# Attention before two MLP layers: queries stored like keys, and one transpose for the last 64 queries and keys of a pair of heads

## The chip, the cores and the metric

One NeuronCore of a Trainium2 chip runs the whole program as one launch. The metric is the device time of one execution in microseconds (us). Before the change it is 1063.98 us, the median of three runs (1063.94, 1063.98, 1067.12).

## What is computed

The reference is attention with capped scores, whose output is the input of two MLP layers (called moe and moe2 there):

```
scores = cap * tanh((q @ k^T / sqrt(64)) / cap)
attn   = exp(scores) / sum(exp(scores))
x  = attn @ v                 # [4 batches, 12 heads, 448, 64], then laid out as 1792 tokens x 768
h  = x @ w_in                 # 768 -> 2048
x  = (h - tanh(h)) @ w_out    # 2048 -> 768
h  = x @ w_in2
out = (h * sigmoid(1.702 h)) @ w_out2
```

There are 4 x 12 = 48 heads of 448 queries and 448 keys, each with 64 elements. All inputs that matter here are fp32.

## The kernel before

The attention stage works on 24 pairs of heads, numbered g = 0 to 23 (`NG = 24`); a pair puts 2 x 64 = 128 features on the partitions. For a pair it does the following.

- `load_qk(g)` (L458) loads queries and keys as rows into a tile `raw`. The queries stand in 112 partitions with 4 consecutive rows of each head in a partition (`C = 4`, `CP = 112`). The first 384 keys stand in 128 partitions with 3 rows each (`KC = 3`), and the last 64 keys (`KT = 64`) in 64 partitions. That is five DMAs: two for the queries (L466), two for the keys (L472), one for the last 64 keys (L476). All are issued by SyncE (SP), one after the other; of pair 0 alone, one query load, one key load and the load of the last keys are issued by ScalarE. Three `raw` tiles exist, so `load_qk(g)` may start once the transposes of pair g - 3 are through.
- `prep_q(g)` (L500) transposes the four query blocks of 112 rows on TensorE (L506) into one PSUM bank, and VectorE copies 448 columns to the first half of a tile `qk` (L90). `prep_k(g)` (L509) transposes three key blocks of 128 rows (L515) and the block of 64 rows (L516), and another copy fills the second half.
- `scores` (L519) multiplies a block of 128 keys with all queries, separately for the two heads: 64 partitions each (L527). `tail_scores` (L530) does the last 64 keys of two pairs together (L537). ScalarE applies tanh and exp (L546, L548). `pair_pv` (L561) multiplies with the values (L568), and `sums_of_two` (L570) adds up the exponentials (L575).
- `load_v` (L485) loads the values of a pair in two DMAs (`rv` and `vt`).

The order on each engine follows the program for all that is wrapped in `pin`. In the loop over g (L648), the transposes of pair g + 3 stand in iteration g: ahead of `scores(g + 1, 0)` where g is even, and ahead of `pair_pv(g, 0)` where g is odd. Pairs 0, 1 and 2 are prepared ahead, and iteration 1 prepares pairs 3 and 4 right behind each other (L682). The load of pair g + 4 is written in iteration g (L686). TensorE works in this order and waits at the first instruction whose input isn't there.

SP issues all loads and stores of the stage in one queue: beside `raw`, `rv` and `vt` these are the weights of the first MLP layer (`wd`, L190, converted by ScalarE at L205 and VectorE at L214 and L220), the converted weights that are kept (`kept`, L241), attention output for later (`xd`, L586), the sums (`wrow`, L604) and their inverses read back as rows (`wb`, L610), which VectorE multiplies with at L655. The order in which SP issues them is set by the scheduler when the program is built.

The order of a pair's queries goes through the whole kernel as the order of the tokens. It is undone when the result is stored: `rows_out` (L1210) takes a block of 128 tokens and cuts it where a run of 112 ends, so every block is stored in two DMAs, each to rows 4 apart.

Of the kernel before, what the change touches and what calls it, by code (L numbers as in the profile page):

```python
# [9 lines left out]
F32 = mybir.dt.float32  # L10
# [30 lines left out]
def attention_moe_moe(ctx, tc, q, k, v, cap, w_in1, w_out1, w_in2, w_out2, out):  # L41
    nc = tc.nc
    B, H, S, D = q.shape
    DM, DF = w_in1.shape
    P = 128
    C = 4
    CP = S // C
    KC = S // P
    KT = S - KC * P
    NP = H // 2  # L50
    KM = DM // P
    KF = DF // P
# [4 lines left out]
    HW = DM // 2  # L57
# [19 lines left out]
    def pin(ins):  # L77
        return tc.keep_in_program_order(ins) if pinned[0] else ins
# [10 lines left out]
    def hi_dve(dst, src):  # L89
        pin(nc.vector.tensor_copy(out=dst, in_=src))  # L90
# [4 lines left out]
    ident = const.tile([P, P], F32, name="ident")  # L95
# [9 lines left out]
    xd = [dr_p.tile([P, TOKENS[1]], F32, name=f"xd{i}") for i in range(KM)]  # L105
    wrow = [dr_p.tile([4, NP // 2, n], F32, name=f"wrow{p}") for p, n in enumerate(TOKENS)]
    x_big = big.tile([P, 2 * KM * TOKENS[0]], F32R, name="x")
# [5 lines left out]
    def first_pool(name, bufs, **kw):  # L113
        return first.enter_context(tc.tile_pool(name=name, bufs=bufs, **kw))

    one_p = first_pool("one", 1)
    raw_p = first_pool("raw", 3)
# [12 lines left out]
    SR = P // 4  # L130
    sel = one_p.tile([P, NP // 2, SR], F32, name="sel")
    vt = [one_p.tile([P, P], F32, name=f"vt{i}") for i in range(4)]
# [228 lines left out]
    def add(out, a, kind, b):  # L361
        nc.vector.tensor_tensor(out=out, in0=a, in1=b, op=kind)  # L362
# [82 lines left out]

    NG = B * NP
    raw, rawv, qkt = {}, {}, {}
# [10 lines left out]
    def load_qk(g, second=None):  # L458
        if g >= NG:
            return  # L460
        b, hp = divmod(g, NP)
        t = raw_p.tile([P, 2, 2 * C * D], F32, tag="raw", name="raw")
        queues = (nc.sync, second or nc.sync)
        for j in range(2):
            a = slice(j * D, (j + 1) * D)
            queues[j].dma_start(  # L466
                out=t[:CP, 0].rearrange("p (c e) -> p c e", c=C)[:, :, a],
                in_=q[b, 2 * hp + j].rearrange("(p c) d -> p c d", c=C),
            )
        for j in range(2):  # L470
            a = slice(j * D, (j + 1) * D)
            queues[j].dma_start(  # L472
                out=t[:, 1].rearrange("p (c e) -> p c e", c=C)[:, :KC, a],
                in_=k[b, 2 * hp + j, :KC * P].rearrange("(p c) d -> p c d", c=KC),
            )
        queues[1].dma_start(  # L476
            out=t[:KT, 1, KC * P:].rearrange("p (h d) -> p h d", h=2),
            in_=k[b, 2 * hp:2 * hp + 2, KC * P:].rearrange("h p d -> p h d"),
        )
        raw[g] = t  # L480

    def tail_rows(g):
        return slice(g % 2 * KT, (g % 2 + 1) * KT)

    def load_v(g):  # L485
        if g >= NG:
            return
        b, hp = divmod(g, NP)
        tv = rv_p.tile([P, 2, KC, D], F32, tag="rv", name="rv")
# [10 lines left out]
    def prep_q(g):  # L500
        if g >= NG:
            return
        qkt[g] = st_p.tile([P, 2 * S], F32, tag="qk", name="qk")
        ps = ps_s.tile([P, 512], F32, tag="s", name="ps_qk")
        for c in range(C):
            pin(nc.tensor.transpose(ps[:, c * CP:(c + 1) * CP], raw[g][:CP, 0, c * P:(c + 1) * P], ident[:CP, :CP]))  # L506
        hi_dve(qkt[g][:, :S], ps[:, :S])

    def prep_k(g):  # L509
        if g >= NG:  # L510
            return
        ps = ps_s.tile([P, 512], F32, tag="s", name="ps_qk")
        t = raw.pop(g)
        for c in range(KC):
            pin(nc.tensor.transpose(ps[:, c * P:(c + 1) * P], t[:, 1, c * P:(c + 1) * P], ident))  # L515
        pin(nc.tensor.transpose(ps[:, KC * P:S], t[:KT, 1, KC * P:], ident[:KT, :KT]))  # L516
        (hi_act if g == 0 else hi_dve)(qkt[g][:, S:], ps[:, :S])

    def scores(g, c):  # L519
        if g >= NG:  # L520
            return
        ps = ps_b.tile([P, 2, 512], F32, tag="b", name="ps_sc")
        qk = qkt[g]
        kc = slice(S + c * P, S + (c + 1) * P)
        for j in range(2):
            a = slice(j * D, (j + 1) * D)
            pin(nc.tensor.matmul(ps[:, j, :S], qk[a, kc], qk[a, :S], start=True, stop=True))  # L527
        sc_t[g, c] = ps

    def tail_scores(g):  # L530
        if g >= NG:
            return
        ps = ps_b.tile([P, 2, 512], F32, tag="b", name="ps_tl")
        for n in (g, g + 1):
            for j in range(2):
                a = slice(j * D, (j + 1) * D)
                pin(nc.tensor.matmul(  # L537
                    ps[tail_rows(n), j, :S], qkt[n][a, S + KC * P:], qkt[n][a, :S], start=True, stop=True
                ))
        sc_t[g, KC] = ps  # L540

# [28 lines left out]
    def sums_of_two(g):  # L570
        b, p = divmod(g // 2, NP // 2)
        if p == 0:
            sum_t[b] = ps_r.tile([P, 512], F32, tag="r", name="ps_r")
        for n in range(4):
            pin(nc.tensor.matmul(  # L575
                sum_t[b][n * SR:(n + 1) * SR, :S], sel[:, p], ts_t[g + n // 2][:, n % 2],
                start=(p == 0), stop=(p == NP // 2 - 1),
            ))
# [38 lines left out]
    def attention():  # L617
# [5 lines left out]
        def x_part(n):  # L623
            b, i = divmod(n, NP)
            n = S if b == 0 else CUT
            return i, n, slice(b * S, b * S + n)

        load_qk(0, nc.scalar)
        nc.sync.dma_start(out=capr, in_=cap.partition_broadcast(P))
        nc.vector.tensor_scalar(  # L630
            out=cpos.bitcast(U32), in0=capr.bitcast(U32), scalar1=0x7FFFFFFF, scalar2=None, op0=ALU.bitwise_and
        )
        nc.vector.reciprocal(out=tsc, in_=cpos)
        nc.vector.tensor_scalar(out=tsc, in0=tsc, scalar1=QK_SCALE, scalar2=None, op0=ALU.mult)
        load_qk(1)
        load_v(0)
        load_qk(2)
        load_v(1)

        def prep(g):  # L640
            prep_q(g)
            prep_k(g)
# [110 lines left out]
    def part_of(tag, name="part"):  # L753
        return temp_p(tag).tile([P, NT if tag == "t" else TC], F32, tag=tag, name=name)[:, :TOKENS[now[0]] // 2]
# [455 lines left out]
    def rows_out(half, n, ps, plus=None, two=False):  # L1210
        tag = ("q", "v", "t", "far")[n % 4]
        o = part_of(tag, "o")[:, :HW]
        if plus is None:
            nc.scalar.copy(out=o, in_=ps[:, :HW])
        else:
            add(o, ps[:, :HW], ALU.add, plus)
        a0 = a = FIRST[now[0]] + n * P
        while a < a0 + P:
            z = min((a // CP + 1) * CP, a0 + P)
            s, c = divmod(a // CP, C)  # L1220
            p0 = a % CP
            dst = out[s * S:(s + 1) * S, half * HW:(half + 1) * HW].rearrange("(p c) e -> c p e", c=C)
            q = nc.scalar if two and a > a0 else nc.sync
            q.dma_start(out=dst[c, p0:p0 + z - a], in_=o[a - a0:z - a0])
            a = z

    def x_load(h, i):
# [104 lines left out]
```

## Time and profile before

| | |
|---|---|
| median of three runs | 1063.98 us |
| the profiled execution | 1063.42 us |
| its span, first to last instruction | 1061.6 us |
| TensorE (PE) busy | 1051.6 us, 99% |
| VectorE (DVE) busy | 811.6 us, 76% |
| ScalarE (ACT) busy | 692.3 us, 65% |
| GpSimd (POOL) busy | 54.5 us, 5% |
| shares of the chain that ended last | PE 92%, DVE 3%, DMA 1%, ACT 1% |
| of these, by line | L506 1%, L515 1%, L527 5%, L568 7% |

The attention stage takes about the first 200 us; the MLP layers take the rest. The profiled execution is 0.56 us faster than the median. A busy time counts an engine as busy while any of its instructions runs. TensorE's weight loads stand apart as PEld. Names such as `ps_qk` or `raw` are those of the program's tiles.

### The profile page before, as it was taken

The page shows a single profiled execution, that of the slowest core. Times are in us where ns is not written, and L with a number is a line of the kernel's source. Part 1 is how long each engine was busy: PE and PEld are TensorE (multiplying, and loading weights), DVE is VectorE, ACT ScalarE, POOL GpSimd, SP SyncE. Part 2 cuts the span into 40 slices and gives each one's busy share as a digit, 9 for nine tenths or more (in the row PEclk, how much of TensorE's full clock was granted, in tenths as well). Part 3 has the DMA queues.
Part 4 walks back from the last instruction along what each step waited for, and adds up shares of the span by engine and source line. Part 5 has one row for each costly group of instructions (what it writes and reads, how often), then busy time and mean ns, then how long its engine had stood idle before and what let it go on. Part 6 is the DMA issues. An engine that isn't in the chain of part 4 may idle for free.

```text
span 1061.6 us, 15403 instructions
## 1 busy us (share of the span) xinstructions
PE 1051.6 (99%) x5483; PEld 860.4 (81%) x5483; DVE 811.6 (76%) x1089; ACT 692.3 (65%) x958; POOL 54.5 (5%) x56
## 2 busy tenths in 40 slices
PE   9999999999999999999999999999999999999998
PEld 3333333699999998888878888887899999999998
DVE  4688979799985525988999998576799973448973
ACT  6898898798863425656785756655755755557663
POOL 0013243200000000000000000000000000000000
PEclk9999999999999999999999999999999999999999
DMA  6877668675577878887874853799654554444443
GB/s 145 210 204 210 193 185 239 202 245 212 190 241 246 296 247 267 280 300 247 274 232 144 272 191 90 262 320 301 226 166 132 182 160 125 136 120 142 150 136 103
DMA packets 153749, 218.17 MB, mean 206 GB/s; under 512 B 58380, under 2 KB 101704, under 8 KB 153672
## 3 DMA queue, kind: packets, MB, share of 16 engines
q1 hardware_dynamic: 152376, 216.58, 64.7%
q8 instruction: 43, 0.70, 0.3%
q10 hardware_dynamic: 1296, 0.61, 0.2%
q14 instruction: 34, 0.28, 0.1%
HBM read 158.86 MB, written 58.28 MB: 205 GB/s over the span
## 4 chain that ended last, share of the span: by engine, by line
PE 92%; DVE 3%; DMA 1%; ACT 1%; issue 1%; SPq 0%; DVEq 0%; ACTq 0%
PE ps_o L1182 19%; PE ps_h L900 19%; PE ps_h L1080 18%; PE ps_y L940 9%; PE ps_y L993 9%; PE ps_pv L568 7%; PE ps_sc L527 5%; PE ps_qk L506 1%; PE ps_tl L537 1%; PE ps_r L575 1%; PE ps_qk L515 1%; DMA wd<-in_moe_w_in_dram 1%; DVE wl L93 1%; DVE gr L800 0%; PE wps L1276 0%
## 5 line engine op out<-in xcount | busy, mean ns | idle before, releaser
L81 ACT CAST rh<-gr 128x512 fp32r<-128x512 f32 (+1 forms) x179 | 103.6, 584 | 101.8 <-PE ps_o L1182 63.3
L900 PE MATMUL ps_h<-x,wh 128*128 128x384 f32 (+1 forms) x672 | 152.9, 358 | 0.0
L93 DVE TENSOR_TENSOR rl<-gr,rh 128x512 fp32r<-128x512 f32 (+1 forms) x179 | 113.3, 638 | 25.7 <-ACT rh L81 24.8
L1182 PE MATMUL ps_o<-wh,rl 128*128 128x384 f32 x392 | 130.9, 334 | 0.0
L1182 PE MATMUL ps_o<-wh,rh 128*128 128x384 f32 x392 | 130.9, 334 | 0.0
L1182 PE MATMUL ps_o<-wl,rh 128*128 128x384 f32 x392 | 130.9, 334 | 0.0
L900 PEld LDWEIGHTS ps_h<-x,wh 128*128 128x128 f32 x672 | 121.1, 188 | 12.0 <-issue 0.7
L93 DVE TENSOR_TENSOR wl<-whole,wh 128x768 fp32r<-128x768 f32 (+1 forms) x103 | 93.7, 910 | 14.9 <-ACT wh L81 14.0
L81 ACT CAST wh<-whole 128x768 fp32r<-128x768 f32 (+1 forms) x103 | 82.4, 800 | 23.1 <-PE ps_h L1080 10.6
L1080 PE MATMUL ps_h<-x,wh 128*128 128x384 f32 (+1 forms) x336 | 97.2, 359 | 0.0
L900 PE MATMUL ps_h<-x,wl 128*128 128x384 f32 (+1 forms) x384 | 88.1, 364 | 0.0
L546 ACT ACTIVATE t<-ps_sc,tsc 128x896 f32<-128x896 f32 x72 | 69.8, 1004 | 22.4 <-PE ps_sc L527 22.4
L900 PEld LDWEIGHTS ps_h<-x,wl 128*128 128x128 f32 x384 | 69.8, 188 | 9.7 <-issue 1.4
L1182 PEld LDWEIGHTS ps_o<-wh,rh 128*128 128x128 f32 x392 | 73.6, 188 | 0.0
L1182 PEld LDWEIGHTS ps_o<-wl,rh 128*128 128x128 f32 x392 | 73.6, 188 | 0.0
L1182 PEld LDWEIGHTS ps_o<-wh,rl 128*128 128x128 f32 x392 | 73.6, 188 | 0.0
L548 ACT ACTIVATE t<-t,cpos 128x896 f32<-128x896 f32 x72 | 72.3, 1042 | 0.4
L1080 PE MATMUL ps_h<-x,wl 128*128 128x512 f32 (+1 forms) x192 | 69.5, 362 | 0.0
L362 DVE TENSOR_TENSOR gr<-gr 128x512 f32<-128x512 f32 (+2 forms) x112 | 68.9, 640 | 0.7 <-DMA gr<-xa 0.4
L527 PE MATMUL ps_sc<-qk 64*128 64x448 f32 x288 | 67.9, 570 | 0.8 <-ACT qk L81 0.6
L362 DVE TENSOR_TENSOR part<-ps_h,part 128x512 f32<-128x512 f32 (+1 forms) x48 | 29.8, 621 | 50.6 <-PE ps_h L1080 50.5
L220 DVE SCALAR_TENSOR_TENSOR wr<-wr,wd 128x768 uint32<-128x768 uint32 x48 | 46.1, 961 | 27.8 <-ACT wd L212 21.4
(154 smaller groups left out, 2193.9 us busy)
## 6 DMA issues: line engine op xcount, KB each, us to landing
wd<-in_moe_w_in_dram SPq DMA_DIRECT2D x64, 384.0 KB
wd<-in_moe_w_out_dram SPq DMA_DIRECT2D x29, 768.0 KB
whole<-single SPq DMA_DIRECT2D x36, 384.0 KB
whole<-s SPq DMA_DIRECT2D x33, 384.0 KB
wh<-kept SPq DMA_DIRECT2D x25, 384.0 KB
wl<-kept SPq DMA_DIRECT2D x25, 384.0 KB
single<-wr SPq DMA_DIRECT2D x24, 384.0 KB
whole<-t SPq DMA_DIRECT2D x22, 384.0 KB
```

What stands on the lines that cost most here:

```text
L81: pin(nc.scalar.copy(out=dst, in_=src))
L93: return pin(nc.vector.tensor_tensor(out=dst, in0=src, in1=hi.bitcast(F32), op=ALU.subtract))
L362: nc.vector.tensor_tensor(out=out, in0=a, in1=b, op=kind)
L527: pin(nc.tensor.matmul(ps[:, j, :S], qk[a, kc], qk[a, :S], start=True, stop=True))
L546: pin(nc.scalar.activation(out=t, in_=ps[:, :, :S], func=AF.Tanh, scale=tsc))
L548: ins = pin(nc.scalar.activation(out=tt[g, c], in_=tt[g, c], func=AF.Exp, scale=cpos))
L568: pin(nc.tensor.matmul(ps[a, :S], w, t[:, j], start=(c == 0), stop=(c == KC - 1)))
L900: pin(nc.tensor.matmul(ps, w[:, kk, :], x[kk][:, a], start=(m == 0), stop=(m == len(seq) - 1)))
L940: nc.tensor.matmul(bank[e][:, :a1 - a0], w[:, kk, c], x[2 * j + kk][:, a0:a1], start=(j == 0 and m == 0), stop=(j == KF // 2 - 1 and m == ...
L993: nc.tensor.matmul(ps[e], w[:, kk, c], x, start=(name == head and k == 0 and m == 0), stop=(k == KH - 1 and m == 2), skip_group_check=True,)
L1080: nc.tensor.matmul(ps, w, x, start=(name == head and m == 0), stop=(m == len(seq) - 1), skip_group_check=True,)
L1182: nc.tensor.matmul(ps[n], x[:, t], w[:, kk, :], start=(first and k == 0 and m == 0), stop=(k == KH - 1 and m == 2), skip_group_check=True,)
```

## The change

Queries are laid out as the keys are: 384 queries in 128 partitions with 3 rows each, and the last 64 apart. The last 64 queries and the last 64 keys of a pair share one block of `raw`: queries in partitions 0 to 63, keys in 64 to 127. One transpose of 128 x 128 turns both, so a pair has seven transposes of one shape where it had eight of three shapes. The first PSUM bank now holds 512 columns (448 queries and the 64 last keys) and the second 384. A pair's load has six DMAs where it had five, since the last queries are loaded by themselves; of pair 0, the load of the last keys moves from ScalarE's queue to SP's, and that of the last queries takes its place. `rows_out` cuts its blocks of 128 tokens at 128, 256, 384 and 448 of a batch, so 56 stores become 44.

```diff
-    C = 4
-    CP = S // C
     KC = S // P
     KT = S - KC * P
+    KQ0 = S + KT
...
-        t = raw_p.tile([P, 2, 2 * C * D], F32, tag="raw", name="raw")
+        t = raw_p.tile([P, 2 * KC + 1, 2 * D], F32, tag="raw", name="raw")
         queues = (nc.sync, second or nc.sync)
-        for j in range(2):
-            a = slice(j * D, (j + 1) * D)
-            queues[j].dma_start(
-                out=t[:CP, 0].rearrange("p (c e) -> p c e", c=C)[:, :, a],
-                in_=q[b, 2 * hp + j].rearrange("(p c) d -> p c d", c=C),
+        for n, (x, c0) in enumerate(((q, 0), (k, KC + 1))):
+            for j in range(2):
+                queues[j].dma_start(
+                    out=t[:, c0:c0 + KC, j * D:(j + 1) * D],
+                    in_=x[b, 2 * hp + j, :KC * P].rearrange("(p c) d -> p c d", c=KC),
+                )
+            queues[1 - n].dma_start(
+                out=t[n * KT:(n + 1) * KT, KC].rearrange("p (h d) -> p h d", h=2),
+                in_=x[b, 2 * hp:2 * hp + 2, KC * P:].rearrange("h p d -> p h d"),
             )
...
-        for c in range(C):
-            pin(nc.tensor.transpose(ps[:, c * CP:(c + 1) * CP], raw[g][:CP, 0, c * P:(c + 1) * P], ident[:CP, :CP]))
-        hi_dve(qkt[g][:, :S], ps[:, :S])
+        for c in range(KC + 1):
+            pin(nc.tensor.transpose(ps[:, c * P:(c + 1) * P], raw[g][:, c], ident))
+        hi_dve(qkt[g][:, :KQ0], ps)
...
-            pin(nc.tensor.transpose(ps[:, c * P:(c + 1) * P], t[:, 1, c * P:(c + 1) * P], ident))
-        pin(nc.tensor.transpose(ps[:, KC * P:S], t[:KT, 1, KC * P:], ident[:KT, :KT]))
-        (hi_act if g == 0 else hi_dve)(qkt[g][:, S:], ps[:, :S])
+            pin(nc.tensor.transpose(ps[:, c * P:(c + 1) * P], t[:, KC + 1 + c], ident))
+        (hi_act if g == 0 else hi_dve)(qkt[g][:, KQ0:], ps[:, :KC * P])
...
-        kc = slice(S + c * P, S + (c + 1) * P)
+        kc = slice(KQ0 + c * P, KQ0 + (c + 1) * P)
...
-                    ps[tail_rows(n), j, :S], qkt[n][a, S + KC * P:], qkt[n][a, :S], start=True, stop=True
+                    ps[tail_rows(n), j, :S], qkt[n][a, S:KQ0], qkt[n][a, :S], start=True, stop=True
...
-            z = min((a // CP + 1) * CP, a0 + P)
-            s, c = divmod(a // CP, C)
-            p0 = a % CP
-            dst = out[s * S:(s + 1) * S, half * HW:(half + 1) * HW].rearrange("(p c) e -> c p e", c=C)
+            s, t = divmod(a, S)
+            c = t // P
+            z = min(s * S + min((c + 1) * P, S), a0 + P)
+            dst = out[s * S:(s + 1) * S, half * HW:(half + 1) * HW]
+            if c < KC:
+                dst = dst[:KC * P].rearrange("(p c) e -> c p e", c=KC)[c]
+                t -= c * P
             q = nc.scalar if two and a > a0 else nc.sync
-            q.dma_start(out=dst[c, p0:p0 + z - a], in_=o[a - a0:z - a0])
+            q.dma_start(out=dst[t:t + z - a], in_=o[a - a0:z - a0])
```

On TensorE, VectorE, ScalarE and GpSimd the instructions stand in the same order as before, with the shapes changed and one transpose less per pair. The place on TensorE where iteration 1 prepares pairs 3 and 4 (`raw_380` and `raw_386`) before `pair_pv(1, 0)` reads, before:

```order
L506 MATMUL ps_qk_426<-ident_75,raw_380 128x112 x4
L515 MATMUL ps_qk_432<-ident_75,raw_380 128x128 x3
L516 MATMUL ps_qk_432<-ident_75,raw_380 128x64
L506 MATMUL ps_qk_439<-ident_75,raw_386 128x112 x4
L515 MATMUL ps_qk_445<-ident_75,raw_386 128x128 x3
L516 MATMUL ps_qk_445<-ident_75,raw_386 128x64
L568 MATMUL ps_pv_451<-t_407,rv_306 64x448 x2
```

With the change (pair 4 is `raw_387` there, and lines are those of the changed file) it reads:

```order
L499 MATMUL ps_qk_428<-ident_75,raw_380 128x128 x4
L508 MATMUL ps_qk_434<-ident_75,raw_380 128x128 x3
L499 MATMUL ps_qk_440<-ident_75,raw_387 128x128 x4
L508 MATMUL ps_qk_446<-ident_75,raw_387 128x128 x3
L560 MATMUL ps_pv_451<-t_409,rv_309 64x448 x2
```

The transpose of the last keys is gone from the end, and the fourth of the first four reads the last queries and last keys together.

On SP, the start of the queue before (the loads of pairs 0 and 1, `raw_281` and `raw_291`, the cap, and the values of pair 0):

```order
L466 DMA raw_281<-in_q_dram 112x4x64
L472 DMA raw_281<-in_k_dram 128x3x64
L629 DMA capr_80<-in_cap_dram 128x1
L466 DMA raw_291<-in_q_dram 112x4x64 x2
L472 DMA raw_291<-in_k_dram 128x3x64 x2
L476 DMA raw_291<-in_k_dram 64x2x64
```

and the loads of pairs 3 and 4 further on, before:

```order
L466 DMA raw_380<-in_q_dram 112x4x64 x2
L472 DMA raw_380<-in_k_dram 128x3x64 x2
L476 DMA raw_380<-in_k_dram 64x2x64
L466 DMA raw_386<-in_q_dram 112x4x64 x2
L472 DMA raw_386<-in_k_dram 128x3x64 x2
L476 DMA raw_386<-in_k_dram 64x2x64
L494 DMA vt3_144<-in_v_dram 64x2x64
L190 DMA wd_460<-in_moe_w_in_dram 128x3x256
```

The same loads of pairs 3 and 4 with the change:

```order
L465 DMA raw_380<-in_q_dram 128x3x64 x2
L469 DMA raw_380<-in_q_dram 64x2x64
L465 DMA raw_380<-in_k_dram 128x3x64 x2
L469 DMA raw_380<-in_k_dram 64x2x64
L465 DMA raw_387<-in_q_dram 128x3x64 x2
L469 DMA raw_387<-in_q_dram 64x2x64
L465 DMA raw_387<-in_k_dram 128x3x64 x2
L469 DMA raw_387<-in_k_dram 64x2x64
L487 DMA vt3_144<-in_v_dram 64x2x64
L465 DMA raw_454<-in_q_dram 128x3x64 x2
```

Each load has one issue more, at its third place, and the load of the last keys stays its last issue. The first load of weights `wd`, which stood behind `vt3`, now comes after the load of pair 5 (`raw_454`) and the values of pair 3.

## Rows read from the trace of the kernel before

**Rows 1.** Windows by stage: busy us (instructions) of PE, PEld, DVE, ACT, POOL; PEclk; DMA.

```profile
24.00:116.00 92.00, 92.00 (x516) 33.96 (x514) 71.58 (x86) 79.73 (x86) 21.55 (x16) 1.00 0.73 202
```

**Rows 2.** Chain that ended last, in order of time: start, us, what.

```profile
62.02 0.90 PE ps_pv L568 x4
...
77.73 0.90 PE ps_pv L568 x4
```

**Rows 3.** Timeline of PE, even iteration, windows cut at 64.1 and 64.6: start, us, instruction.

```profile
63.74 0.60 PE L506 MATMUL ps_qk<-ident,raw 112*128 112x112 f32 x4
63.89 0.45 PE L506 MATMUL ps_qk<-ident,raw 112*128 112x112 f32 x3
64.18 0.49 PE L515 MATMUL ps_qk<-ident,raw 128*128 128x128 f32 x3
64.40 0.27 PE L515 MATMUL ps_qk<-ident,raw 128*128 128x128 f32 x1
64.60 0.27 PE L516 MATMUL ps_qk<-ident,raw 64*128 64x64 f32 x1
65.61 0.97 PE L568 MATMUL ps_pv<-tl,vt 128*64 128x448 f32 x4
```

**Rows 4.** Timeline of PE, the odd iteration that follows.

```profile
69.72 0.60 PE L506 MATMUL ps_qk<-ident,raw 112*128 112x112 f32 x4
...
70.78 0.97 PE L568 MATMUL ps_pv<-t,rv 128*64 128x448 f32 x4
71.69 1.02 PE L527 MATMUL ps_sc<-qk 64*128 64x448 f32 x4
72.64 0.98 PE L537 MATMUL ps_tl<-qk 64*64 64x448 f32 x8
```

**Rows 5.** Timeline of SP, 12 to 26 us: start, us of issuing, DMA.

```profile
13.85 1.25 SPq L466 DMA_DIRECT2D raw<-in_q_dram  x2
...
19.84 0.63 SPq L476 DMA_DIRECT2D raw<-in_k_dram  x1
20.57 0.62 SPq L494 DMA_DIRECT2D vt<-in_v_dram  x1
```

**Rows 6.** Timeline from 2 us: one small DMA and who waited for it.

```profile
2.26 0.80 SPq L629 DMA_DIRECT2D capr<-in_cap_dram  x1
...
5.41 0.15 DVE L630 TENSOR_SCALAR cpos<-capr 128x1 uint32<-128x1 uint32 x1 [4.26 <-DMA capr<-in_cap_dram]
```

**Rows 7.** Timeline of SP, 78 to 87 us.

```profile
79.06 1.25 SPq L604 DMA_DIRECT2D wrow<-w  x4
...
81.97 0.50 SPq L610 DMA_DIRECT2D wb<-wrow  x1
```

**Rows 8.** Timeline of PE, 20 to 26 us: pair 4, and what follows.

```profile
22.42 0.60 PE L506 MATMUL ps_qk<-ident,raw 112*128 112x112 f32 x4 [0.18 <-DVE qk L90]
...
23.63 0.97 PE L568 MATMUL ps_pv<-t,rv 128*64 128x448 f32 x4
```

**Rows 9.** Timeline of ACT, 33 to 34.5 us: the first weights are converted.

```profile
33.54 0.91 ACT L205 ACTIVATE wr<-wd 128x768 f32<-128x768 f32 x1
```

**Rows 10.** Timeline, 137 to 150 us: SP, and VectorE's use of `wb`.

```profile
140.83 1.15 SPq L476 DMA_DIRECT2D raw<-in_k_dram  x1
142.02 1.24 SPq L610 DMA_DIRECT2D wb<-wrow  x2
...
148.10 0.48 DVE L655 TENSOR_TENSOR xs<-xs,wb 128x320 f32<-128x320 f32 x1
```

**Rows 11.** Timeline of PE at the start: warm-up matmuls, and pair 0.

```profile
1.19 4.87 PE L1276 MATMUL wps<-wz 128*128 128x512 bf16 x11 [1.19 <-DVE cub_u L1283]
...
5.85 0.95 PE L506 MATMUL ps_qk<-ident,raw 112*128 112x112 f32 x4
6.60 0.68 PE L515 MATMUL ps_qk<-ident,raw 128*128 128x128 f32 x3
```

**Rows 12.** Timeline of ACT, 1054 to 1062 us: the last store.

```profile
1058.06 0.38 ACTq L1224 DMA_DIRECT2D out_dram<-o  x1
```

More of the change, by code (lines that the diff above doesn't have):

```diff
@@ L461, in load_qk @@
         b, hp = divmod(g, NP)
-        t = raw_p.tile([P, 2, 2 * C * D], F32, tag="raw", name="raw")
+        t = raw_p.tile([P, 2 * KC + 1, 2 * D], F32, tag="raw", name="raw")
         queues = (nc.sync, second or nc.sync)
-        for j in range(2):
-            a = slice(j * D, (j + 1) * D)
-            queues[j].dma_start(
-                out=t[:CP, 0].rearrange("p (c e) -> p c e", c=C)[:, :, a],
-                in_=q[b, 2 * hp + j].rearrange("(p c) d -> p c d", c=C),
-            )
[L470 to L479, printed above, removed]
+        for n, (x, c0) in enumerate(((q, 0), (k, KC + 1))):
[7 more added lines that the diff above has]
+                in_=x[b, 2 * hp:2 * hp + 2, KC * P:].rearrange("h p d -> p h d"),
+            )
         raw[g] = t
```

## Prediction

> **What bounds the kernel now.** I read the windows by stage first. In the attention stage past its start TensorE is busy for 92.00 of 92.00 us [rows 1], while ScalarE, next in line, has 79.73. A busy TensorE need not be the limit, so the chain of waits comes next: from 62.02 to 77.73 it stays on TensorE, and that is one period of two pairs, 15.71 us [rows 2]. So in this stretch every tenth of a microsecond that TensorE saves or waits goes into the total, as long as ScalarE, at 79.73 / 92.00 of the time, keeps its slack. Then I read TensorE's timeline around the transposes, since what they cost is read from start to start and not from their durations, and last SP's timeline, since each pair gets one DMA more.
>
> **What TensorE saves.** In an even iteration the four query transposes start at 63.74, the second at 63.89, the first key transpose at 64.18, the third at 64.40, the odd-shaped one at 64.60, and the values' matmuls behind the scores at 65.61 [rows 3]. So the first step is 0.15, a step with 112 columns is (64.18 - 63.89) / 3 = 0.10, one with 128 columns (64.40 - 64.18) / 2 = 0.11, and from the last full transpose to an instruction of another tile shape it is 0.20. Seven of one shape take 0.16 + 5 x 0.11 = 0.71 to the start of the seventh, and 0.20 more until something of another shape starts: 0.91.
>
> - Odd iteration: before, 69.72 to 70.78, which is 1.06 [rows 4]. The saving is 0.15.
> - Even iteration: before, 63.74 to 65.61, which is 1.87. Here the odd-shaped transpose had already paid for the scores' change of tile shape: it started 0.20 late, and scores have 64 rows too. With the change, scores pay it themselves: 0.91, plus 0.95 for scores that follow another shape (71.69 to 72.64 in [rows 4]), is 1.86. The saving is 0.01.
>
> Pairs 5 to 23 are prepared in nine odd and ten even iterations: 9 x 0.15 + 10 x 0.01 = 1.45 us, and I take 1.5. A step read as 0.105 instead of 0.11 makes it 1.8; if four wider query transposes need another 0.02, it is 1.3. Those are its bounds. What pairs 0 to 4 save is not added, for the reason that comes next.
>
> **What the extra DMA costs at the start.** Each load has one issue more on SP. From 13.85 to 20.57 SP issues ten DMAs without a pause: 0.67 us each [rows 5]. In this stretch it is SP that is behind. The last issue of pair 4's load is at 19.84 [rows 5], and its transposes run at 22.42 [rows 8]. With the change five more issues stand ahead of it: the last keys of pair 0, which come over from ScalarE's queue, and the last queries of pairs 1 to 4. 5 x 0.67 = 3.35, so it is issued at 23.19.
>
> How long until it lands, no row says for this transfer. One end is the cap, issued at 2.26 and waited for until 5.41: 3.15 us [rows 6]. The other is the sums, whose fourth issue is at about 80.0 and which are read back at 81.97: at most 1.97 us [rows 7]. I take 2.4, nearer to the second, which also runs beside other traffic. So the load is complete at 25.6 (25.2 to 26.4). The Trainium skill, page DMA: Bandwidth & Descriptors, section Anatomy of one DMA, gives a fixed 2.0 us plus the bytes at 436 GB/s, for the GpSimd path. By that figure 32 KB would be there after an estimated 2.08 us, and the sum below would be 0.3 us smaller; the cap's row is a full microsecond above it, and the measurement decides.
>
> Before, the last keys were needed by the eighth transpose. Now they are needed by the fourth, which would start at 22.42 + 0.15 + 2 x 0.10 = 22.77. It waits until 25.6 instead. Behind it stand three key transposes and a change of shape, 3 x 0.11 + 0.20 = 0.53, so the values' matmuls start at 26.1 and not at 23.63 [rows 8]: 2.5 us later (2.0 to 3.3). Queued behind the waiting transpose on TensorE are the values of pair 1 and the scores of pair 2, whose inputs are all there, and ScalarE waits for those scores. As TensorE has no slack afterwards [rows 1], none of it is won back. Whatever pairs 0 to 3 win or lose is swallowed here, because the wait ends when SP gets there; SP doesn't wait for TensorE at this place, since pair 4 takes the buffer of pair 1.
>
> **What costs nothing.** The copies move 512 + 384 columns where they moved 448 + 448. The first weights are issued later: seven issues for pair 5 and values, two for the weights, from 23.86, so at about 30, and 33.2 in SBUF by the larger of the two latencies; ScalarE converts them at 33.54 [rows 9] plus 2.5. That covers it by 2.8 us; without the cover ScalarE would wait, which has slack itself. Twelve stores fewer lie in a stage where SP waits for the results. The last store, issued at 1058.06 [rows 12], carries 64 rows where it carried 96: I count 0.1 us for it, at least nothing, at most 0.3.
>
> **Sum.** 2.5 - 1.5 - 0.1 = +0.9 us on the profiled execution's 1063.42, which is 1064.3. That execution lies 0.56 below the median of the runs, 1063.98, so in terms of medians I expect **1064.9**, with 1064.1 to 1065.9 from the bounds of the terms. The measurement can tell about 0.3%, 3.2 us, from no change; this is within it.
>
> **Rivals.**
>
> - *SP keeps up (chance 0.12).* If the new small DMAs issue faster than 0.67, or pair 4 isn't late, the saving stands alone: 1063.98 - 1.6 = 1062.4. Against it: SP issues back to back in [rows 5], and the load of 64 rows there takes 0.63, like the larger ones.
> - *SP falls behind a second time (0.17).* In the second half of attention SP is busy too: the last issue of a load takes 1.15 at 140.83, and `wb` is issued at 142.02 to 143.26 and used by VectorE at 148.10 [rows 10]. Its second issue is at 142.6, 5.5 us ahead; less a latency of 3.15, it has 2.3 to spare, 3.5 by the shorter one. SP waited for the sums up to 81.97 [rows 7] and can make up there what came before; from then on pairs 14 to 20 put seven more issues ahead of `wb`, 4.7 us, while VectorE by then is 2.5 less about 1.3 later, 1.2 us. That leaves 0 to 1.2 of a wait if SP takes up nothing, and TensorE, which waits for VectorE's copies, loses it; with the longer issues of this stretch, or with what SP is late already, up to 2.5. I price it at 1.5: 1066.4. For it: no slack is visible on SP around 140. [...]
> - *TensorE's clock falls in the wait: slower (0.13).* TensorE would stand still from 23.1 to 25.6 with only transposes on either side. At the start, four query transposes took 6.60 - 5.85 = 0.75 [rows 11] against 0.44 later [rows 3]: the engine was at the lower level (1.2 GHz, not 2.4), after work from 1.19 on. So coming back took at least 6.60 - 1.19 = 5.4 us of work, half of it lost: 2.7. If the wait brings the clock down, the total is 1067.6, 0.34% above. It decides from about 2.3 us of loss on. Against it: the granted clock is 1.00 throughout the stage [rows 1]; but TensorE has no wait of that length there. The Trainium skill, page TensorE: Matmul & The Clock Gate, section Why this matters for your kernels, says that idle gaps between bursts of matmuls send the clock back to the lower level; by that rule this rival is possible, and no run here has shown such a gap.
>
> **How the numbers follow.** The forecast has 0.58, the rivals 0.12, 0.17 and 0.13. The range that should hold 8 in 10 goes down to SP keeping up, 1062.4 (half of that case lies below), and up to 1067.4, which leaves out more than half of the clock's case and the worst of SP's second lag. Slower by over 0.3% (above 1067.2): 0.03 of the forecast's share, half of the clock's and a third of the second lag, 0.15 in all. Faster by over 0.3% (below 1060.8) needs twice the saving and no wait: 0.03. The rest, 0.82, is within 0.3%.
>
> **What would show it.** On TensorE: seven transposes with 0.11 between their starts, 0.9 from the first of them to the matmuls of another shape in odd iterations, and a period of two pairs of 15.71 - 0.16 = 15.55. At pair 4: a wait for `raw` of 2 to 3 us between 22.5 and 26, and six issues per load on SP at 0.67. The granted clock should stay at 1.00 behind that wait. Wrong would be: no wait at pair 4, a period that hasn't changed, waits of VectorE for `wb` or of TensorE for `raw` between 100 and 165 us, or a lower clock from 23 us on.

## The result, and the profile after

The changed kernel takes **1075.48 us**, the median of five runs (1073.36 to 1076.36); before it was 1063.98. The ratio of the means is 1.0097, with a 95% interval of 1.0081 to 1.0113: slower by 1%, or 11.5 us by the medians, where 0.9 us was forecast, and outside the range. Of the five runs of the kernel before, one took 3706.64 us and is left out of the ratio; the others took 1063.33 to 1067.12. The profiled execution took 1076.36 us, with a span of 1074.5 us; it lies 12.9 us above the profiled execution of before.

What was meant to get cheaper did get cheaper, and by the amount worked out. TensorE's timeline of the changed kernel around pairs 8, 9 and 10, where L499 and L508 are the transposes, L560 the values, L519 the scores:

```profile
57.77 0.66 PE L499 MATMUL ps_qk<-ident,raw 128*128 128x128 f32 x4
58.27 0.49 PE L508 MATMUL ps_qk<-ident,raw 128*128 128x128 f32 x3
58.69 0.97 PE L560 MATMUL ps_pv<-t,rv 128*64 128x448 f32 x4
...
67.36 0.66 PE L499 MATMUL ps_qk<-ident,raw 128*128 128x128 f32 x4
67.85 0.49 PE L508 MATMUL ps_qk<-ident,raw 128*128 128x128 f32 x3
68.27 1.02 PE L519 MATMUL ps_sc<-qk 64*128 64x448 f32 x4
69.22 0.97 PE L560 MATMUL ps_pv<-tl,vt 128*64 128x448 f32 x4
...
73.33 0.66 PE L499 MATMUL ps_qk<-ident,raw 128*128 128x128 f32 x4
```

An odd iteration needs 58.69 - 57.77 = 0.92 us from the first transpose to the next shape, where [rows 4] had 1.06. An even one needs 69.22 - 67.36 = 1.86, where [rows 3] had 1.87. Two pairs take 73.33 - 57.77 = 15.56, against 15.71 [rows 2].

The loss comes from waits, and from TensorE's clock behind them. Three windows of the changed kernel, in the columns of [rows 1] (PEclk is the granted clock, as a share of full speed):

```profile
22.00:30.00 8.00, 5.31 (x23) 1.75 (x23) 4.88 (x7) 2.68 (x3) 0.00 (x0) 0.81 0.41 91
30.00:40.00 10.00, 10.00 (x57) 3.64 (x55) 3.68 (x6) 9.03 (x10) 0.00 (x0) 0.98 0.78 218
140.00:160.00 20.00, 17.28 (x90) 6.06 (x86) 14.93 (x18) 15.29 (x17) 8.61 (x7) 0.92 0.68 202
```

The last window of the three, in the kernel before:

```profile
140.00:160.00 20.00, 20.00 (x118) 7.37 (x114) 14.86 (x21) 18.02 (x20) 9.51 (x9) 1.00 0.70 195
```

TensorE stands idle for 2.7 us in the first window and for 2.7 us in the third, and in both the granted clock is under 1.00, which it is not before, here and in [rows 1]. The places are the loads of pairs 4 and 20. TensorE's timeline there (in brackets the idle time ahead of a group, and what ended it):

```profile
22.77 0.52 PE L499 MATMUL ps_qk<-ident,raw 128*128 128x128 f32 x3 [1.06 <-DMA raw<-in_q_dram]
25.21 0.30 PE L499 MATMUL ps_qk<-ident,raw 128*128 128x128 f32 x1 [1.92 <-DMA raw<-in_k_dram]
...
25.95 0.97 PE L560 MATMUL ps_pv<-t,rv 128*64 128x448 f32 x4
26.86 1.84 PE L519 MATMUL ps_sc<-qk 64*128 64x448 f32 x4
```

```profile
151.97 0.55 PE L499 MATMUL ps_qk<-ident,raw 128*128 128x128 f32 x3
155.25 0.33 PE L499 MATMUL ps_qk<-ident,raw 128*128 128x128 f32 x1 [2.72 <-DMA raw<-in_k_dram]
...
156.78 1.87 PE L519 MATMUL ps_sc<-qk 64*128 64x448 f32 x4
```

In both, the fourth transpose, the one that reads the last 64 queries and keys, waits for its rows. Behind each wait four score matmuls take 1.84 and 1.87 us where the same four take 1.02 (68.27 above): that is the lower of the two clock levels, 1.2 GHz and not 2.4. By the granted clock alone this costs (1 - 0.81) x 8 + (1 - 0.98) x 10 = 1.7 us behind pair 4 and (1 - 0.92) x 20 = 1.6 us behind pair 20. So there are two losses at each place, a wait and a clock. The values of pair 1 start at 25.95 and not at 23.63 [rows 8], 2.32 us later; what the lower clock adds is measured below as well (a_fill).

VectorE's waits between 84 and 204 us show the same lateness on another engine (us in all, how often, the longest). First the kernel before, then the changed one:

```profile
DVE xs L655 <- DMA wb<-wrow: 0.6, 1, 0.6
```

```profile
DVE xs L647 <- DMA wb<-wrow: 8.3, 5, 2.7
```

And SP, which issues all of it. The load of pair 4 on its timeline, the sums, their first use, the first `wb` of the second half, and the last issue of pair 20's load:

```profile
19.43 1.21 SPq L465 DMA_DIRECT2D raw<-in_q_dram  x2
20.69 0.63 SPq L469 DMA_DIRECT2D raw<-in_q_dram  x1
21.36 1.27 SPq L465 DMA_DIRECT2D raw<-in_k_dram  x2
22.67 0.62 SPq L469 DMA_DIRECT2D raw<-in_k_dram  x1
...
85.86 1.29 SPq L596 DMA_DIRECT2D wrow<-w  x4
...
90.36 0.49 SPq L602 DMA_DIRECT2D wb<-wrow  x1
...
142.76 1.11 SPq L602 DMA_DIRECT2D wb<-wrow  x2
...
151.12 0.69 SPq L469 DMA_DIRECT2D raw<-in_k_dram  x1
```

Six issues per load at 0.65 us each, as forecast. But the sums are written at 85.86, 6.8 us later than before (79.06, [rows 7]), while TensorE is only 3.3 to 3.6 us later there (pairs 14 and 10); and the last issue of pair 20's load stands at 151.12 where it stood at 140.83 [rows 10], 10.3 us later. The row of 140.83, whose pair the prediction doesn't name, is the load of pair 20.

The table follows the starts of a pair's first query transpose, in us against the trace of before (below zero is earlier), for the changed kernel and the experiments. The last two columns are the first matmul of the first MLP layer and the last matmul of the kernel.

| | pair 3 | 4 | 5 | 16 | 20 | 21 | 23 | first MLP | last |
|---|---|---|---|---|---|---|---|---|---|
| changed kernel | -0.6 | +0.4 | +3.9 | +3.1 | +3.4 | +7.8 | +7.7 | +9.1 | +13.0 |
| b_sixth | -0.2 | +1.1 | +1.9 | +10.2 | +10.0 | +10.0 | +10.0 | +11.0 | +12.9 |
| b_three | -0.7 | -0.7 | -0.7 | -0.7 | -0.7 | -0.7 | -0.7 | -0.7 | +1.0 |
| a_four | -1.4 | -1.2 | -1.5 | -2.3 | -2.4 | -2.5 | -2.7 | -2.6 | -0.7 |
| a_pool | -0.7 | -0.6 | +0.1 | -0.7 | -0.8 | -0.9 | -1.1 | -1.0 | -0.1 |
| a_four_early | -0.9 | -0.8 | -1.1 | -1.9 | -1.7 | +2.6 | +2.5 | +4.3 | +6.2 |
| a_four_late | -0.4 | +0.7 | +4.0 | +3.3 | +3.2 | +3.0 | +2.8 | +2.9 | +5.3 |
| a_mid | -0.5 | +0.5 | +3.9 | +3.1 | +3.0 | +3.0 | +4.4 | +6.7 | +5.9 |
| a_last | -0.3 | +0.9 | +4.4 | +3.6 | +3.5 | +3.3 | +3.2 | +3.2 | +6.9 |
| a_fill | -0.6 | +0.7 | +2.8 | +2.0 | +2.5 | +6.9 | +6.8 | +10.3 | +16.7 |
| a_fill2 | -0.5 | +0.8 | +3.6 | +2.8 | +3.2 | +7.4 | +7.4 | +9.3 | +11.0 |

In its first row the 13.0 us come about as follows: 4.5 from pair 3 to pair 5, 4.4 from pair 20 to pair 21, 1.4 between pair 23 and the first MLP matmul (VectorE waits 2.7 us for `wb` once more there, and TensorE waits 1.3 us ahead of the last values, at 204.04, which it did not before; that the one brings the other was not tested), 3.9 in the MLP layers; 0.6 is won at the start, and from pair 5 to 20 and 21 to 23 another 0.7 net. In the MLP layers the other profiles of the table lie -0.8 to +6.4 off the one profile of before, `b_three` +1.6 with TensorE's attention work unchanged, so some 2 us of the 3.9 may be scatter between executions. The changed kernel has one more wait there, and a granted clock of 0.94 from 540 to 570 us:

```profile
555.36 0.50 PE L985 MATMUL ps_y<-rh,wl 128*128 128x512 f32 x1 [1.91 <-DVE wl L92]
...
556.30 0.63 PE L985 MATMUL ps_y<-rh,wl 128*128 128x512 f32 x1
```

No experiment looked into that third place.

### The profile page after: what moved, and what is told of

Same layout as the page of the kernel before. It is cut to its first block, busy times and chain, and to the rows that moved or that the text cites. A ratio compares the mean times of both kernels' runs of the same rounds, so it can differ in the third digit from the quotient of the medians.

```text
span 1074.5 us, 15384 instructions
## 1 busy us (share of the span) xinstructions
PE 1054.7 (98%) x5459; PEld 860.8 (80%) x5459; DVE 815.4 (76%) x1089; ACT 692.9 (64%) x958; POOL 56.8 (5%) x56
## 3 DMA queue, kind: packets, MB, share of 16 engines
q1 hardware_dynamic: 152680, 216.67, 64.1%
## 5 line engine op out<-in xcount | busy, mean ns | idle before, releaser
L519 PE MATMUL ps_sc<-qk 64*128 64x448 f32 x288 | 69.1, 584 | 0.7 <-ACT qk L80 0.6
L985 PE MATMUL ps_y<-rh,wl 128*128 128x512 f32 x168 | 66.2, 394 | 1.9 <-DVE wl L92 1.9
```

The lines of the kernel that those rows point to most:

```text
L985: nc.tensor.matmul(ps[e], w[:, kk, c], x, start=(name == head and k == 0 and m == 0), stop=(k == KH - 1 and m == 2), skip_group_check=True,)
```

## Experiments

**The theory, and its rivals.** Theory 1: SP issues about one DMA per 0.66 us, and the sixth issue of each load makes the loads late, first at pair 4 and again around pair 20; the clock falls behind the waits. Against it: that the new shapes (rows of 64, wider copies, a transpose of mixed rows) cost something by themselves, or that the clock alone is the cause.

The first four kernels ran against before at 1064.88 us (median of 19 runs, 1061.32 to 1068.13).

**b_sixth: the kernel before, with one DMA more per load and nothing else of the change.** The last 64 queries are loaded once more, into a tile that nobody reads.

```diff
+        extra = ex_p.tile([KT, 2 * D], F32, tag="ex", name="ex")
+        nc.sync.dma_start(
+            out=extra.rearrange("p (h d) -> p h d", h=2),
+            in_=q[b, 2 * hp:2 * hp + 2, KC * P:].rearrange("h p d -> p h d"),
+        )
```

> The kernel before, plus one load more per pair on SyncE: the last 64 queries are loaded a second time, into a tile that nobody reads. Transposes, layout and stores are those of before. Theory 1 (the number of issues on SyncE is what costs): the last keys of pair 4 are issued 4 x 0.67 = 2.7 us later, the eighth transpose waits about 1.5 us for them near 23.4, and near 150 us a second wait of about 3 us follows; with the lower clock behind one or both of them, 1068 to 1076 us. Theory 2 (the new shapes cost: the last keys are needed by the fourth transpose, the transfers are cut otherwise): nothing of that is here, 1064 to 1065 us.

Measured: 1076.5 us (1071.5 to 1079.52, 4 runs), ratio 1.0099 [1.0064, 1.0134], just above the range of theory 1. That is a loss as large as that of the change with none of its shapes. TensorE's timeline has the wait at pair 4, and one behind pair 14; below it stands the window around the second:

```profile
23.53 0.57 PE L512 MATMUL ps_qk<-ident,raw 112*128 112x112 f32 x4 [1.48 <-DMA raw<-in_q_dram]
24.84 0.52 PE L521 MATMUL ps_qk<-ident,raw 128*128 128x128 f32 x3 [0.74 <-DVE qk L90]
...
109.44 1.76 PE L574 MATMUL ps_pv<-t,rv 128*64 128x448 f32 x4 [4.06 <-DVE xs L90]
```

```profile
100.00:120.00 20.00, 15.16 (x66) 4.83 (x62) 16.58 (x18) 10.28 (x12) 9.62 (x7) 0.83 0.73 195
```

VectorE waits for `wb` here too, 10.3 us in all. From pair 14 to pair 16 TensorE slips by 7.4 us: the wait of 4.06, and (1 - 0.83) x 20 = 3.4 by the clock. So the second loss comes earlier than in the changed kernel, by way of VectorE and `wb` and not of `raw`: SP's lateness is common to both kernels, the place where it breaks through is not fixed.

**a_four: the changed kernel with four issues per load.** From pair 1 on, the main queries of both heads come in one DMA, and the main keys.

```diff
+            if g > 0:
+                nc.sync.dma_start(
+                    out=t[:, c0:c0 + KC].rearrange("p c (j d) -> p c j d", j=2),
+                    in_=x[b, 2 * hp:2 * hp + 2, :KC * P].rearrange("j (p c) d -> p c j d", c=KC),
+                )
```

> The changed kernel with four loads per pair instead of six: the two heads of the 384 queries in one DMA, and those of the keys, to the same places with the same 256-byte runs; pair 0 as before. Theory 1 (number of issues): pair 4's load is issued 5 us earlier, no wait at pair 4 nor near 150 us, granted clock 1.00 throughout; what stays is TensorE's saving of 1.5 us or a little more, 1061 to 1062.5 us. Theory 2 (new shapes): the fourth transpose still waits for the load that is issued last, and the time stays above 1070 us.

Measured: **1062.28 us** (1059.74 to 1063.94, 10 runs), ratio 0.9972 [0.9956, 0.9988]: faster than both kernels. Its SP and its TensorE at pair 4:

```profile
15.85 0.62 SPq L465 DMA_DIRECT2D raw<-in_q_dram  x1
16.51 0.68 SPq L475 DMA_DIRECT2D raw<-in_q_dram  x1
17.23 0.62 SPq L465 DMA_DIRECT2D raw<-in_k_dram  x1
17.89 0.68 SPq L475 DMA_DIRECT2D raw<-in_k_dram  x1
```

```profile
21.19 0.65 PE L505 MATMUL ps_qk<-ident,raw 128*128 128x128 f32 x4 [0.46 <-DVE qk L89]
21.68 0.52 PE L514 MATMUL ps_qk<-ident,raw 128*128 128x128 f32 x3
22.13 0.97 PE L566 MATMUL ps_pv<-t,rv 128*64 128x448 f32 x4
```

A DMA of twice the size is issued in 0.62 us, no longer than one of the single size. SP gets ahead (the last issue of pair 4's load stands at 17.89 and not at 22.67), nothing waits for `raw`, and the values start at 22.13, before the 23.63 of [rows 8].

**b_three: the kernel before, with the same merge** (three issues per load).

> The kernel before with three loads per pair instead of five (both heads in one DMA for queries and for keys), and nothing else of the change. Both theories: before hardly waits for a load, so 1063 to 1064 us. It is the partner of the four-load version: their difference is what the seven transposes of one shape are worth without waits, 1.5 us by the sum of the prediction, at most 2.

Measured: 1065.91 us (1063.95 to 1069.65, 10 runs), ratio 1.0006 [0.999, 1.0023]: no change. Before, SP had just enough room, so fewer issues alone bring nothing. The difference of the two rows of the table, a_four less b_three, is then what the transposes save: -0.7 at pair 3, -2.0 at pair 23, which is 1.35 from pair 3 to pair 23, and 1.2 of it from pair 5 on. By the medians the two kernels differ by 3.6 us, where at most 2 was expected; their runs scatter over 4.2 and 5.7 us, and the two traces end 1.6 us apart.

**a_fill: the changed kernel, with zeros multiplied in the wait at pair 4.** Eleven matmuls into a bank of their own ahead of the fourth query transpose; this is added work.

```diff
+            if g == 4 and c == KC:
+                fill = ps_r.tile([P, 512], F32, tag="r", name="fill")
+                for _ in range(11):
+                    pin(nc.tensor.matmul(fill, wz[:, :P], wz, start=True, stop=True))
```

> The changed kernel with 11 matmuls of zeros (bf16, 512 columns) on TensorE ahead of the fourth query transpose of pair 4, that is inside the wait for its load; their result isn't used. If the lower clock behind the wait is its own price: the wait ends when it did (25.2), the granted clock stays 1.00 between 22 and 40 us, and pair 5 is prepared 1.7 us earlier than in the changed kernel, 1073.5 to 1074 us. If the clock has nothing to do with the gap: the same clock dip, 1075 to 1076 us.

Measured: 1077.13 us (1073.73 to 1080.05, 4 runs), ratio 1.0108 [1.0075, 1.0142], no better in the total. Its trace, which is of the slowest of the four, shows the clock at 1.00 from 22 to 40 us:

```profile
23.49 2.54 PE L502 MATMUL fill<-wz 128*128 128x512 bf16 x11
25.86 0.27 PE L503 MATMUL ps_qk<-ident,raw 128*128 128x128 f32 x1
```

From the fourth transpose of pair 4 (25.86) to the first of pair 5 (35.06) it takes 9.20 us, where the changed kernel took 25.21 to 36.24, 11.03. So the clock's price at this place is 1.8 us, and it comes of the wait. Pair 5 is prepared only 1.2 us earlier than in the changed kernel, where 1.7 was expected: the rows were there at 25.26, and the zeros held TensorE up to 25.86. What was won there was lost elsewhere: the wait at pair 20 and its clock are unchanged, the granted clock falls twice more (0.79 from 204 to 212 us, 0.89 from 750 to 765), and the MLP layers end 16.7 us later than before the change.

The next four ran against before at 1064.52 us (16 runs, 1059.76 to 1066.46).

**a_four_early and a_four_late: four issues per load in pairs 1 to 4 alone, or from pair 5 on.**

```diff
-            if g > 0:
+            if 0 < g < 5:
```

```diff
-            if g > 0:
+            if g > 4:
```

> The changed kernel, with both heads' main queries in one DMA and the main keys in one (four issues per load) for pairs 1 to 4 alone; from pair 5 on six issues per load as in the changed kernel. Theory A (each of the two lags of SyncE is made where it is seen, by the issues of its own stretch, because in between SyncE waits for rows that TensorE's progress makes): the wait at pair 4 and the clock dip behind it are gone, so pair 5 starts about 1.4 us earlier than before the change instead of 3.9 later, but the wait at pair 20 and the dip behind it come all the same (pair 20 to pair 21 slips by about 4.4); end of the attention about +2 to +4 against before, median near 1069. Theory B (the second lag is the first one carried on): without the first there is no second, pair 23 starts about 2.7 earlier than before, median near 1062.5, as with four issues throughout.

> The changed kernel, with four issues per load from pair 5 on and six for pairs 0 to 4. Theory A: the wait at pair 4 (about 2.3) and the dip behind it stay, pair 5 starts 3.9 later than before; from there two pairs win 0.15 each time and nothing slips at pair 20 or behind pair 23: pair 23 about +2.6, median near 1067 to 1068. Theory B (the first lag alone sets off the rest): a second wait at pair 20 comes here too, pair 23 at +7, median above 1071.

Measured: early 1069.57 us (1068.84 to 1070.34, 5 runs), ratio 1.0045 [1.003, 1.0059]; late 1068.02 us (1062.89 to 1069.45, 6 runs), ratio 1.0025 [1.0005, 1.0046]. Each takes away its own half: in the early one pair 5 is 1.1 us early, and pair 20 to 21 slips by 4.3 all the same; in the late one pair 5 is 4.0 late, and nothing slips behind. The early kernel, at the wait that stayed, and its windows:

```profile
150.04 0.33 PE L505 MATMUL ps_qk<-ident,raw 128*128 128x128 f32 x1 [2.62 <-DMA raw<-in_k_dram]
```

```profile
22.00:30.00 8.00, 8.00 (x46) 2.70 (x44) 4.99 (x7) 6.30 (x8) 0.00 (x0) 1.00 0.63 175
...
140.00:160.00 20.00, 17.38 (x89) 6.07 (x88) 15.13 (x18) 14.59 (x16) 9.09 (x8) 0.91 0.73 206
```

So of theory A this holds: the second loss is not the first one carried on. Its reason, that SP catches up in between, is taken up with a_mid and a_last.

**a_pool: six DMAs per load as in the change, but the sixth issued by GpSimd.**

```diff
-            queues[1 - n].dma_start(
+            (nc.gpsimd if n and second is None else queues[1 - n]).dma_start(
```

> The changed kernel with the same six DMAs per load, but the sixth (the last 64 keys of both heads) issued by GpSimd instead of SyncE, pair 0 excepted. If it is SyncE's issue time, and not one more DMA in the queues or small rows landing late, that makes the loads late: no wait at pair 4 and none at pair 20, pair 23 about 1.5 to 2.7 earlier than before, median 1062 to 1064. If it is the DMA itself (its descriptors, its landing): the waits for the raw tile stay, median about 1075. A third outcome: GpSimd, busy 9 to 11 of 20 us between 100 and 120 us in the changed kernel, issues late itself: a wait for the tail of the raw tile at pairs 14 to 20 and none at pair 4, median between.

Measured: 1064.01 us (1061.81 to 1064.63, 10 runs), ratio 0.9998 [0.9984, 1.0012]. The loss is gone though every byte and every DMA of the change is there. SP with its five issues of pair 4's load, GpSimd with the sixth, then TensorE:

```profile
17.77 1.22 SPq L465 DMA_DIRECT2D raw<-in_q_dram  x2
19.03 0.62 SPq L469 DMA_DIRECT2D raw<-in_q_dram  x1
19.70 1.27 SPq L465 DMA_DIRECT2D raw<-in_k_dram  x2
```

```profile
10.02 0.58 POOL L469 DMA_DIRECT2D raw<-in_k_dram  x1 [1.94 <-PE ps_qk L508]
```

```profile
21.82 0.66 PE L499 MATMUL ps_qk<-ident,raw 128*128 128x128 f32 x4 [0.46 <-DVE qk L89]
23.32 0.52 PE L508 MATMUL ps_qk<-ident,raw 128*128 128x128 f32 x3 [0.85 <-DMA raw<-in_k_dram]
23.77 0.97 PE L560 MATMUL ps_pv<-t,rv 128*64 128x448 f32 x4
```

GpSimd issues the sixth as soon as the transposes of pair 1 are through, long before SP gets to the other five. A wait of 0.85 is left at pair 4, for the keys that SP issues, and none at pair 20; pair 23 is 1.1 us early, where 1.5 to 2.7 was expected. What was late was SP, by the time that its issues take. The Trainium skill, page DMA: Bandwidth & Descriptors, section Issuing engines are not separate DMA queues, says that DMAs of all issuers share the same 16 engines, and that issuing from several saves only the issuer's time, "usually small relative to the DMA itself". No run here shows the sharing by itself. That the issuer's time is what can be saved agrees with this pair of kernels; that it is small holds here for a single DMA (0.6 us against 2.5 from the last issue of pair 4's load, at 22.67, to its use at 25.21), but the sum of issues was the limit.

**a_fill2: zeros in both waits** (40 small matmuls each, into the bank that the transpose then writes; added work).

```diff
+            if g in (4, 20) and c == KC:
+                for _ in range(40):
+                    pin(nc.tensor.matmul(ps[:, c * P:], wz[:, :P], wz[:, :P], start=True, stop=True))
```

> The changed kernel with 40 matmuls of zeros (128 columns, bf16) ahead of the fourth query transpose of pairs 4 and 20, so that TensorE runs through most of the two waits. They add work, and the loads land no earlier, so the waits still end when the last 64 rows land. If the stretches at half clock behind the waits come of the waits: the granted clock stays at 1.0 between 22 and 40 us and between 140 and 165 us, and each of the slips (pair 4 to 5: 3.6 in the changed kernel; pair 20 to 21: 4.4) shrinks by about 1.5, to 2.1 and 2.9. If the dips have another cause, both stay.

Measured: one run, 1074.3 us. TensorE behind the two waits:

```profile
26.64 0.30 PE L502 MATMUL ps_qk<-ident,raw 128*128 128x128 f32 x1 [0.70 <-DMA raw<-in_k_dram]
...
28.11 1.02 PE L522 MATMUL ps_sc<-qk 64*128 64x448 f32 x4
```

```profile
156.40 0.33 PE L502 MATMUL ps_qk<-ident,raw 128*128 128x128 f32 x1 [1.93 <-DMA raw<-in_k_dram]
...
157.89 1.02 PE L522 MATMUL ps_sc<-qk 64*128 64x448 f32 x4
```

The scores take 1.02 again, and the granted clock reads 1.00 from 22 to 30 us and from 140 to 160 us. But the slips were half right only: 3.6 became 2.8 (not 2.1) and 4.4 became 4.2 (not 2.9), because the rows landed later, at 26.5 and 156.35 and not at 25.08 and 155.20. From the fourth transpose of pair 20 to pair 21 it is 9.3 us against 10.8: 1.6 for the clock at this place. Why the rows came later in this one execution stays open.

The last two ran against before at 1064.58 us (11 runs, 1062.22 to 1068.74).

**a_mid and a_last: four issues for pairs 5 to 13 alone, or for pairs 14 to 23 alone** (`if 4 < g < 14:`, `if g > 13:`). They ask from where on SP's second lag builds up.

> The changed kernel with four issues per load for pairs 5 to 13 alone, six for pairs 1 to 4 and 14 to 23. The wait at pair 4 and the clock dip behind it stay in any case (pair 5 about 3.9 later than before the change). Theory C (SyncE's second lag is what the sixth issues of pairs 5 to 20 add up to; SyncE writes the sums late, at 85.86 in the changed kernel against 79.06 before, and catches up with nothing there): 9 x 2 x 0.66 = 12 us of issues less ahead of the sums, they are written when VectorE has them, the margins behind them are those of before less what pairs 14 to 20 add, and nothing waits long: VectorE waits for wb under 2 us in all, no clock dip, pair 23 at about +2.8 to +4, median 1067 to 1070. Theory D (SyncE starts afresh at the sums, and only the issues from pair 14 on count, as the prediction had it): the wait at pair 20 and the 8 us of VectorE's waits for wb stay, pair 23 about +7.7, median about 1075.

> The changed kernel with four issues per load for pairs 14 to 23 alone, six before that. The wait at pair 4 and the dip behind it stay (pair 5 at +3.9). Theory C: the sums are still written some 6 us later than before the change, so VectorE's first use of wb behind pair 10 still waits or has no slack to speak of, but each later pair gives SyncE 1.3 us back, so no wait at pair 20, pair 23 at about +3 to +5, median 1067 to 1070. Theory D: all of the second lag is gone from its start: no wait of VectorE for wb at any use, pair 23 at +2.8, median 1067 to 1068.

Measured: a_mid 1070.54 us (1068.74 to 1077.06, 6 runs), ratio 1.0067 [1.0036, 1.0099]; a_last 1068.16 us (1066.99 to 1070.25, 6 runs), ratio 1.0038 [1.0022, 1.0053]. Neither theory holds whole. In a_mid the sums are written at 82.44, and the wait at pair 20 is gone, as theory C had it; but the issues from pair 14 on bring 5.3 us of VectorE's waits for `wb` back, where C allowed 2, TensorE waits 1.0 us for values (`rv`) at 176.5, and the first MLP matmul is 6.7 us late:

```profile
DVE xs L653 <- DMA wb<-wrow: 5.3, 4, 3.1
```

In a_last the sums are still late (85.50), yet the first use of `wb` has 2 us to spare and no use waits, as theory D had it. What follows: the lag comes from both halves. SP carries what pairs 5 to 13 made it late past the sums, and pairs 14 to 20 use up what is left; the 2.7 us at pair 20 need both, and the second half alone, on top of the wait at pair 4, is enough for a smaller loss. Two of a_mid's runs took 1076.5 and 1077.1; its trace is of 1069.3 and doesn't explain them.

## Why the prediction was wrong

- **What bounds the kernel** was right: whatever TensorE waited stayed in the total, and what it saved came out (a_four).
- **TensorE's saving** was right: 0.15 in an odd iteration (measured 0.14), 0.01 in an even one (0.01), a period of 15.55 (15.56). In all it had 1.5 for pairs 5 to 23, where a_four and b_three differ by 1.2: between pairs 16 and 20 a wait of TensorE for ScalarE, 0.15 us before, grows to 0.37 in a_four and takes 0.2 of it.
- **The wait at pair 4** was right: last issue at 23.19 (22.67), values 2.5 us late (2.32). The load took 2.5 us from its last issue to its use, where 2.4 was taken. That the sum is so close is in part luck: the issue came 0.5 us earlier than counted, and from the waiting transpose to the values it took 0.74 and not 0.53.
- **What costs nothing** held: ScalarE converts the first weights at 37.47, 2.3 us after they land. The last store was not tested by itself; 0.1 us is out of reach in 13.
- **The clock** was taken as unlikely (0.13), on the ground that the granted clock had been 1.00 throughout. As the text said itself, no wait of that length was in that trace, so it could not speak against it. The price was too high: 2.7, against 1.8 and 1.6 measured, since it was read from the start of the kernel, where it counted 5.4 us of work at the lower level. The rule of the Trainium skill, page TensorE: Matmul & The Clock Gate, section Why this matters for your kernels, that idle gaps between bursts of matmuls send the clock back, was borne out at both waits (1.92 and 2.72 us, with a granted clock of 0.81 and 0.92 in their windows). b_sixth shows the limit of it: there the wait at pair 4 fell in two parts, 1.48 and 0.74 us, and its scores behind them took 1.02.
- **SP's second lag** is the step that failed first. It said that SP "can make up there what came before", at the sums, and so counted only the seven sixth issues of pairs 14 to 20, 4.7 us, against a slack of 2.3 to 3.5. SP made up nothing there. It no longer waits for VectorE's sums, as it did for 0.4 us before; it writes them 6.8 us late. Load by load, its last issue is 2.8 us later than before at pair 4, 4.3 at pair 5, 7.6 at pair 14 and 10.3 at pair 20, and TensorE is 3.9, 3.3 and 3.4 us later at pairs 5, 14 and 20. So the load's margin shrank by 0.3, 4.3 and 6.9 us: 4.0 between pairs 5 and 14, where the prediction had nothing, and 2.5 from there to pair 20. Not every issue shows: the 15 sixth issues of pairs 6 to 20 are 9.8 us at 0.65, and 6.5 arrived; where SP took up the rest was not looked into.
- **The place** was wrong too. The rival looked at `wb` alone; at pair 20 TensorE lost its time to `raw`, whose margin the prediction did not read. That load had landed 2.4 us ahead of its use before (146.16, used at 148.53). The wait that this leaves is 4.5 by the difference, and 2.7 was measured, since the rows landed 4.1 us behind the start of their last issue and not 5.3, and the fourth transpose needs them, not the first. a_mid and a_last show both halves of the lag at work.
- **The rivals were handled as alternatives**, each with a chance of its own and a price on top of the forecast. They had one cause, SP's extra issue, and came together: wait and clock at pair 4, wait and clock at pair 20, VectorE's waits for `wb`. With the forecast's own 0.9 that is 0.9 + 1.8 + 4.4 + 1.4 = 8.5 by the end of attention, against 9.1 in the table; no case of the prediction reached above 1067.6. (The bounds of its terms, added straight, give 1063.9 to 1066.0 and not 1064.1 to 1065.9; that decides nothing here.)

## What to carry to other kernels

Where one queue issues everything, price a DMA by its issue, and find the use that has the least margin. Don't take it that the queue starts afresh at a point where it used to wait: SP had waited there for 0.4 us, and with the change it came 6.8 us late. A load that lands 2.4 us ahead of its use has no room for some 15 more issues ahead of it, though only two thirds of their time arrived there. Ask of rivals whether one cause brings several of them, and give that joint case a chance and a time. And when a layout needs more DMAs, first merge others: both heads in one DMA turned a loss of 1% into a gain of 0.3% with the same layout.

## What the runs showed of the hardware

In the rows shown here an issue of a load on SP takes 0.6 to 0.7 us whether it moves one head's 384 rows, both heads', or 64 rows (one in [rows 10] takes 1.15), and GpSimd issues the same small load in 0.58. A wait of 1.9 us with three transposes and another wait of 1.06 ahead of it was followed by TensorE's lower clock level, and so was one of 2.72 us; 2.2 us of waiting in two parts was not (b_sixth), nor was a wait of 1.93 us behind 40 small matmuls (a_fill2).
